# Batch 1's values ahead of w1's second half, another order of the first products, another filler and other places in a kernel of memory attention and a mixture of experts

## The chip, the cores and the metric

The kernel runs on one core of one Trainium2 chip. The time is that of the device in microseconds (us), the median of several runs; smaller is better.

## What is computed

Eight batches of 576 tokens go through an attention over 32 memory slots per head and then through a layer with eight experts, of which each token uses one.

```python
a = exp(phi - max over tokens); a = a / (sum over tokens + 1e-9)
k_m, v_m = einsum('bhsm,bhsd->bhmd', a, k), the same with v
attn = softmax(q @ k_m.T / 8);  x = attn @ v_m          # x: [8, 576, 512]
e(b, s) = argmax(x @ w_gate) if s == 0 or sigmoid(x @ w_local) < 0.5 else e(b, s-1)
out[b, s] = softmax(x @ w_gate)[e] * (relu(x @ w1[e]) @ w2[e])   # w1: 512x1024, w2: 1024x512
```

## The kernel before

For each batch the kernel works with the expert of the batch's first token; which other experts occur is listed along the way, and a loop at the end (`rest`) adds their tokens, if there are any. Since `x` is `attn @ v_m`, the values are multiplied into w1 once per batch: G = v_m @ w1 (`w_pg` makes the product per half of w1, and `w_G` splits it into a high and a low part, `Gh` by ScalarE and `Gl` by VectorE). The first layer (`hidden`) is then attention times G, in three products per head group: `ah`·`Gh`, `ah`·`Gl` and `al`·`Gh`, where `ah` and `al` are the high and low parts of the attention `at`. It first takes 256 tokens in four blocks of 12 products (the first two blocks need the first half of w1, the other two the second half), then 320 tokens in eight blocks of 6. The second layer (`second`, `second_turned`) follows with w2, also in a high and a low part (`w_split`: ScalarE and GpSimd).

Memory and its products. `fetch_phi` and `fetch_kv` load phi, keys and values of a batch; `f_colmax` to `f_exp` make `a`; `f_pkv` ("pkv 0": token groups 0 to 4, "pkv 1": the rest) multiplies it with keys and values; `f_sums` to `f_kvT` normalise and turn the result. All loads are issued by SyncE, in the order of the program.

Order. The kernel is written for a schedule by hand: each engine does its work in the order in which the program names it. `start()` names the work in front of the first block of batch 0: batch 0's memory, its first attention, its expert (`choose`, `expert`), w1 and w2 of that expert (`load1` and `load2`, a half each), batch 1's keys and values, and G of the first half of w1. After that the first and second layer of the batches 0 to 7 follow one another, and all work for the next batches is set between their blocks by the table `PLACES`: for each step and batch a point on a nominal time axis on which each batch has 37.8. The loop at the end runs the blocks, adds each block's nominal length (six products of 256 tokens count 6 x 0.118, of 320 tokens 6 x 0.147, of 512 columns 6 x 0.227) and, after each block, runs all steps whose point has been passed, in the order of their points:

```python
for x in moe(sts[b]):
    now += x
    while places and places[0][0] <= min(now, (b + 1) * END - 0.01):
        _, _, name, n = places.pop(0)
        STEPS[name](sts[n])
```

The four blocks of 256 tokens of batch 0 so end at 1.416, 2.832, 4.248 and 5.664, its first layer at 12.72. Steps that the change touches: "pg 1" and "G 1" (`w_pg` and `w_G` of w1's second half), "pkv 0", "pkv 1", "g pl" and "g lt" (products of the gate and their turning), the softmax of a batch's second half of tokens ("z turn" to "z al", functions `k_turn` to `k_al`), "pl0", "choice" and "expert" (gate of the first token and its expert). "pkv 0" of batch 1 has a filler in front, products of a zero tile into a tile that nobody reads (`warm`).

Of the kernel before, what the change touches and what calls it, by code (L numbers as in the profile page):

```python
# [8 lines left out]
F32 = mybir.dt.float32  # L9
# [17 lines left out]
    "kv": {2: 6.76, 3: 36.1, 4: 68.59, 5: 94.32, 6: 129.4, 7: 168.6},  # L27
    "colmax": {2: 21.1, 3: 55.3, 4: 78.6, 5: 109.2, 6: 147.3, 7: 185.1},
# [8 lines left out]
    "asum": {1: 0.01, 2: 31, 3: 64.8, 4: 92, 5: 127.6, 6: 164.8, 7: 203.2},  # L37
    "pkv 0": {1: 1.34, 2: 30.71, 3: 66.71, 4: 92.5, 5: 127.8, 6: 165.6, 7: 203.7},
    "pkv 1": {1: 4.88, 2: 32.7, 3: 66.71, 4: 94.32, 5: 127.8, 6: 165.6, 7: 203.7},
# [5 lines left out]
    "kv store": {0: 17.59, 1: 15.6, 2: 41.9, 3: 75.4, 4: 98.1, 5: 137.1, 6: 174.4, 7: 212.2},  # L45
    "pgg": {1: 9.9, 2: 44.49, 3: 73.1, 4: 97.61, 5: 135.78, 6: 172.1, 7: 210.8},
    "ggt": {1: 9.9, 2: 44.79, 3: 74.3, 4: 99.7, 5: 135.9, 6: 173.7, 7: 211.5},
# [16 lines left out]
    "choice": {1: 22.9, 2: 54.6, 3: 87.2, 4: 112.5, 5: 149.7, 6: 190.51, 7: 227.3},  # L64
    "expert": {1: 23.1, 2: 54.8, 3: 87.9, 4: 113, 5: 150.2, 6: 190.51, 7: 227.8},
# [38 lines left out]
    "list": {7: 278.9},  # L104
# [8 lines left out]
}  # L113
# [3 lines left out]
def tile_memattn_stickymoe(  # L117
# [12 lines left out]
    nc = tc.nc  # L130
    B, H, S, D = q.shape
    M = phi.shape[3]
    E, DM, F = w1.shape
    P = 128
# [18 lines left out]
    ps_o = ctx.enter_context(tc.tile_pool(name="ps_o", bufs=2, space=PSUM))  # L153
# [153 lines left out]
    def warm(n, cols=512):  # L307

        if not wt or cols < 512:
            wt[0] = ps_o.tile([P, 512], F32, tag="po", name="wp")  # L310
        for _ in range(n):
            if cols > 512:
                nc.tensor.matmul(wt[0], lhsT=zeros, rhs=zeros[:, 0:1].to_broadcast([P, 512]), start=True, stop=True)
                continue
            nc.tensor.matmul(wt[0][:, 0:cols], lhsT=wz[:, 0:P], rhs=wz[:, 0:cols], start=True, stop=True)


# [464 lines left out]
    def w_load1(st, w1e, i, parts=1):  # L782

        w1v = w1e.rearrange("o (h p) f -> p (o h) f", p=P)
        if i == 0:
            st.raw1 = []
        raw = pw.tile([P, HG, F // 2], F32, tag="raw", name="raw1", bufs=3)
        n = F // 2 // parts
        for j in range(parts):
            f0 = F // 2 * i + n * j  # L790
            nc.sync.dma_start(out=raw[:, :, n * j : n * j + n], in_=w1v[:, :, f0 : f0 + n])
        st.raw1.append(raw)

    def w_load2(st, w2e, i):

        w2v = w2e.rearrange("o (c p) d -> p (o c) d", p=P)
        if i == 0:
            st.raw2, st.W2 = [], []
        raw = pw.tile([P, 4, DM], F32, tag="raw", name="raw2", bufs=3)
        for j in (0, 2):  # L800
            nc.sync.dma_start(out=raw[:, j : j + 2], in_=w2v[:, 4 * i + j : 4 * i + j + 2])
        st.raw2.append(raw)
# [258 lines left out]

    def expert(st):

        st.e = nc.values_load(
            st.ei[0:1, 0:1],
            engines=(mybir.EngineType.SP,),
            min_val=0,
            max_val=E - 1,
            skip_runtime_bounds_check_because="an index of the gate's E values",
        )  # L1070

    def load1(st, i, parts=1):
        w_load1(st, w1[bass.ds(st.e, 1)], i, parts)

    def load2(st, i):
        w_load2(st, w2[bass.ds(st.e, 1)], i)

    V = nc.vector
    h, w = pairs
    a, z = PARTS  # L1080
# [25 lines left out]
    def pkv_0(st):  # L1106
        if st.b == 1:
            warm(83, 32)
        f_pkv(st, slice(0, 5))
# [98 lines left out]
    def start():  # L1208
# [50 lines left out]
        expert(s)  # L1259
        load1(s, 0, 2)  # L1260
        load1(s, 1)
        fetch_kv(n, (1,))
        load2(s, 0)
# [75 lines left out]
```

## Time and profile before

| | us |
|---|---|
| runs, median of 3 | 407.85 (407.73 to 408.11) |
| profiled execution, its own time | 406.67 |
| its span, first to last instruction | 404.9 |

The profile shows one execution. Engines: PE is TensorE's matmul, PEld its weight load, DVE VectorE, ACT ScalarE, POOL GpSimd, SP SyncE, which issues the loads. A row of the timeline gives start, duration, engine, line of the kernel, operation, output and inputs by their tile names, shapes and count; in brackets stands the idle time of the engine before it and what ended it. A row of busy windows gives the stretch, its length, the busy time of PE, PEld, DVE, ACT and POOL with the number of instructions, the granted TensorE clock as a share of the full one, the DMA engines' share and GB/s. In the list of waits stand the waiting line, what it waited for, the total, the number and the longest.

In the trace the first block of batch 0 starts at 27.7 us, that of batch 1 at 84.6, that of batch 7 at 359.9, and the last product ends at 398.6.

### The profile page before, as it was taken

What the parts mean: (1) busy time and instruction counts of PE and PEld (TensorE: products, weight loads), DVE (VectorE), ACT (ScalarE), POOL (GpSimd) and SP (SyncE); (2) the same over time, 40 slices, a digit from 0 to 9 for tenths busy, and PEclk for the clock granted to TensorE, in tenths of its full rate; (3) what the DMA queues carried; (4) which work ended last, traced back from release to release, by engine and by line L of the source; (5) the groups of instructions that cost most, each with busy time, mean ns of one, the idle gap of its engine ahead of it and who ended that gap; (6) DMA issues with size and microseconds to landing.
All of it is one profiled execution on the core that took longest, in us unless ns stands there. A gap on an engine that the chain in (4) does not pass through costs nothing.

```text
span 404.9 us, 10638 instructions
## 1 busy us (share of the span) xinstructions
PE 389.3 (96%) x4216; PEld 329.6 (81%) x4216; DVE 286.1 (71%) x718; ACT 177.7 (44%) x436; POOL 151.7 (37%) x164
## 2 busy tenths in 40 slices
PE   7888999999999999999999999999999999999993
PEld 2547878798788877899878997899878996999883
DVE  4588789889977887896877777796867674826300
ACT  2256553446353744337441764245641653255110
POOL 3024442446242851039311771036711741164000
PEclk9999999999999999999999999999999999999998
DMA  7988893989497939899979378944995094302011
GB/s 225 321 296 225 172 378 134 252 197 358 151 305 162 375 107 265 196 389 315 229 198 375 100 202 188 343 189 120 222 223 161 8 307 153 127 0 66 26 54 45
DMA packets 115446, 82.59 MB, mean 204 GB/s; under 512 B 69616, under 2 KB 89088, under 8 KB 115392
## 3 DMA queue, kind: packets, MB, share of 16 engines
q1 hardware_dynamic: 115328, 81.84, 68.3%
q8 instruction: 35, 0.57, 0.6%
q0 software_dynamic: 64, 0.02, 0.2%
q14 instruction: 19, 0.16, 0.1%
HBM read 66.60 MB, written 15.24 MB: 202 GB/s over the span
## 4 chain that ended last, share of the span: by engine, by line
PE 87%; DVE 4%; DMA 4%; SPq 2%; ACT 1%; issue 1%; DVEq 0%; ACTq 0%
PE ph L857 23%; PE po L945 9%; PE po L895 9%; PE po L947 8%; PE po L946 8%; PE po L896 8%; PE po L897 8%; PE pg L824 4%; PE pkv L412 4%; PE psc L533 2%; DMA raw<-in_moe_w_dram 2%; DMA q<-in_q_dram 2%; PE pl L640 1%; DVE h L867 1%; SPq L237 1%; SPq L298 1%
## 5 line engine op out<-in xcount | busy, mean ns | idle before, releaser
L813 POOL TENSOR_TENSOR w2l<-raw,w2h 128x512 fp32r<-128x512 f32 x64 | 82.4, 1307 | 29.1 <-ACT w2h L812 19.3
L857 PE MATMUL ph<-ah,Gh 128*128 128x256 f32 (+1 forms) x256 | 74.2, 305 | 1.2 <-DVE h L867 1.0
L867 DVE SCALAR_TENSOR_TENSOR h<-ph,h 128x320 fp32r<-128x320 f32 (+2 forms) x104 | 52.8, 522 | 31.0 <-ACT h L865 30.3
L857 PE MATMUL ph<-ah,Gl 128*128 128x256 f32 (+1 forms) x256 | 72.1, 296 | 0.1
L945 PE MATMUL po<-h,w2l 128*128 128x320 f32 x224 | 70.8, 316 | 0.0
L946 PE MATMUL po<-h,w2h 128*128 128x320 f32 x224 | 69.2, 309 | 0.0
L947 PE MATMUL po<-h,w2h 128*128 128x320 f32 x224 | 69.2, 309 | 0.0
L865 ACT ACTIVATE h<-ph 128x320 fp32r<-128x320 f32 (+1 forms) x96 | 46.4, 487 | 39.9 <-PE ph L857 39.9
L895 PE MATMUL po<-w2h,h 128*128 128x512 f32 (+1 forms) x152 | 60.0, 394 | 0.0
L896 PE MATMUL po<-w2l,h 128*128 128x512 f32 (+1 forms) x152 | 57.9, 381 | 0.0
L897 PE MATMUL po<-w2h,h 128*128 128x512 f32 (+1 forms) x152 | 57.7, 380 | 0.0
L952 POOL TENSOR_TENSOR oT<-oT,gT 128x320 f32<-128x320 f32 x28 | 20.7, 740 | 95.1 <-DVE oT L951 81.0
L601 POOL TENSOR_TENSOR al<-at,ah 128x576 fp32r<-128x576 f32 (+1 forms) x18 | 23.8, 1327 | 85.9 <-ACT ah L597 75.6
L857 PE MATMUL ph<-al,Gh 128*128 128x256 f32 (+1 forms) x256 | 55.2, 296 | 0.2 <-POOL al L601 0.2
L857 PEld LDWEIGHTS ph<-ah,Gh 128*128 128x128 f32 x256 | 48.4, 189 | 4.9 <-issue 2.1
L857 PEld LDWEIGHTS ph<-ah,Gl 128*128 128x128 f32 x256 | 48.6, 190 | 0.3 <-DVE Gl L839 0.3
L945 PEld LDWEIGHTS po<-h,w2l 128*128 128x128 f32 x224 | 42.1, 188 | 4.4 <-issue 4.0
L812 ACT ACTIVATE w2h<-raw 128x512 fp32r<-128x512 f32 x64 | 38.6, 624 | 9.4 <-PE po L947 8.5
L946 PEld LDWEIGHTS po<-h,w2h 128*128 128x128 f32 x224 | 42.1, 188 | 0.2
L947 PEld LDWEIGHTS po<-h,w2h 128*128 128x128 f32 x224 | 42.1, 188 | 0.0
L857 PEld LDWEIGHTS ph<-al,Gh 128*128 128x128 f32 x256 | 41.4, 190 | 0.4 <-POOL al L601 0.4
L895 PEld LDWEIGHTS po<-w2h,h 128*128 128x128 f32 x152 | 28.6, 188 | 8.2 <-issue 3.0
(163 smaller groups left out, 585.5 us busy)
## 6 DMA issues: line engine op xcount, KB each, us to landing
raw<-in_moe_w_dram SPq DMA_DIRECT2D x34, 512.0 KB, 6.6
raw<-in_moe_w_dram SPq DMA_DIRECT2D x15, 1024.0 KB, 6.2
kv_t<-in_k_dram SPq DMA_DIRECT2D x7, 1152.0 KB, 9.1
kv_t<-in_v_dram SPq DMA_DIRECT2D x7, 1152.0 KB, 11.5
q_t<-in_q_dram SPq DMA_DIRECT2D x112, 72.0 KB, 3.6
att_d<-at SPq DMA_DIRECT2D x8, 576.0 KB, 8.2
out_dram<-oT SPq DMA_DIRECT2D x28, 160.0 KB, 6.4
out_dram<-ot SPq DMA_DIRECT2D x17, 256.0 KB, 4.4
```

The costliest lines, as they stand in the source:

```text
L601: (eng or nc.gpsimd).tensor_tensor(out=st.al[:, gs, ss], in0=st.at[:, gs, ss], in1=st.ah[:, gs, ss], op=ALU.subtract)
L812: nc.scalar.activation(h, src, AF.Copy)
L813: nc.gpsimd.tensor_tensor(out=l, in0=src, in1=h, op=ALU.subtract)
L857: nc.tensor.matmul(pv[:, c - c0], lhsT=lt[:, g, cs], rhs=rt[:, g, s0 : s0 + n], start=(i == 0), stop=(i == 5),)
L865: nc.scalar.activation(hc[:, :, 0:n], pv, AF.Relu)
L867: nc.vector.scalar_tensor_tensor(out=hc[:, :, o : o + z - a], in0=pv[:, :, a:z], scalar=0.0, in1=hc[:, :, a:z], op0=ALU.max, op1=ALU.subtract,
L895: nc.tensor.matmul(po[:, c0:c1], lhsT=h[:, c, th], rhs=hi, start=(c == 0), stop=False)
L896: nc.tensor.matmul(po[:, c0:c1], lhsT=h[:, c, th], rhs=lo, start=False, stop=False)
L897: nc.tensor.matmul(po[:, c0:c1], lhsT=h[:, c, tl], rhs=hi, start=False, stop=(c == FC - 1))
L945: nc.tensor.matmul(po[:, 0:n], lhsT=lo, rhs=h[:, c, 0:n], start=(c == 0), stop=False)
L946: nc.tensor.matmul(po[:, 0:n], lhsT=hi, rhs=h[:, c, 0:n], start=False, stop=False)
L947: nc.tensor.matmul(po[:, 0:n], lhsT=hi, rhs=h[:, c, n : 2 * n], start=False, stop=(c == FC - 1))
```

## The change

In `start()` the load of batch 1's values goes in front of the load of w1's second half. In batch 0, "pg 1", "G 1" and "pkv 0" of batch 1 go from behind the first block to behind the second; the exponential and the sum of the softmax's second half go ahead of "G 1", the steps behind it stay behind; "g pl" goes from behind the fourth block to behind the third, and the first two splits of w2 one block later. The filler of 83 products of 32 columns in bfloat16 becomes one such product and 41 products of 64 rows by 32 columns by one column in FP32 (`burn`). Other points of the table move by little; one definition that stood twice is taken out.

```diff
@@ PLACES
-    "pkv 0": {1: 1.34, 2: 30.71, 3: 66.71, 4: 92.5, 5: 127.8, 6: 165.6, 7: 203.7},
+    "pkv 0": {1: 2.5, 2: 30.71, 3: 66.71, 4: 92.5, 5: 127.8, 6: 165.6, 7: 203.7},
...
-    "pl0": {1: 21.7, 2: 54.5, 3: 86.6, 4: 111.6, 5: 149.4, 6: 190.51, 7: 226.4},
-    "choice": {1: 22.9, 2: 54.6, 3: 87.2, 4: 112.5, 5: 149.7, 6: 190.51, 7: 227.3},
-    "expert": {1: 23.1, 2: 54.8, 3: 87.9, 4: 113, 5: 150.2, 6: 190.51, 7: 227.8},
+    "pl0": {1: 21.7, 2: 54.8, 3: 86.6, 4: 111.6, 5: 149.4, 6: 190.51, 7: 226.4},
+    "choice": {1: 22.9, 2: 54.9, 3: 87.2, 4: 112.5, 5: 149.7, 6: 190.51, 7: 227.3},
+    "expert": {1: 23.1, 2: 55.1, 3: 87.9, 4: 113, 5: 150.2, 6: 190.51, 7: 227.8},
...
-    "z exp": {0: 0.03, 1: 26.8, 2: 54.9, 3: 88.8, 4: 129, 5: 166.2, 6: 203.3, 7: 241.8},
-    "z sum": {0: 0.03, 1: 26.8, 2: 55.4, 3: 88.8, 4: 129.2, 5: 166.6, 6: 203.8, 7: 242.2},
-    "z inv": {0: 0.23, 1: 27.6, 2: 55.4, 3: 88.8, 4: 130.8, 5: 168, 6: 205.6, 7: 244.3},
+    "z exp": {0: 1.5, 1: 26.8, 2: 54.9, 3: 88.8, 4: 129, 5: 166.2, 6: 202.7, 7: 241.8},
+    "z sum": {0: 1.5, 1: 26.8, 2: 55.4, 3: 88.8, 4: 129.2, 5: 166.6, 6: 203.2, 7: 242.2},
+    "z inv": {0: 2.75, 1: 27.6, 2: 55.4, 3: 88.8, 4: 130.8, 5: 168, 6: 205, 7: 244.3},
...
-    "pg 1": {0: 0.13, 1: 32.7, 2: 71.5, 3: 97.6, 4: 139.89, 5: 173, 6: 216.89, 7: 245.61},
-    "G 1": {0: 0.13, 1: 32.8, 2: 71.6, 3: 98.3, 4: 139.89, 5: 175.9, 6: 216.89, 7: 248.3},
-    "g pl": {0: 4.27, 1: 30.72, 2: 61.6, 3: 94.3, 4: 130.8, 5: 168.6, 6: 205.9, 7: 245.6},
+    "pg 1": {0: 2.49, 1: 32.7, 2: 71.5, 3: 97.6, 4: 135.79, 5: 172.11, 6: 210.81, 7: 245.61},
+    "G 1": {0: 2.49, 1: 32.8, 2: 71.6, 3: 98.3, 4: 139.89, 5: 175.9, 6: 216.89, 7: 248.3},
+    "g pl": {0: 3.1, 1: 30.72, 2: 61.6, 3: 94.3, 4: 130.8, 5: 168.6, 6: 205.9, 7: 245.6},
...
@@ tile_memattn_stickymoe
+    def burn(n):
+
+        t = ps_o.tile([P, 512], F32, tag="po", name="wp")
+        for _ in range(n):
+            nc.tensor.matmul(t[0:32, 0:1], lhsT=zeros[0:64, 0:32], rhs=zeros[0:64, 0:1], start=True, stop=True)
...
     def pkv_0(st):
         if st.b == 1:
-            warm(83, 32)
+            warm(1, 32)
+            burn(41)
         f_pkv(st, slice(0, 5))
...
         expert(s)
         load1(s, 0, 2)
+        fetch_kv(n, (1,))
         load1(s, 1)
-        fetch_kv(n, (1,))
         load2(s, 0)
```

The other points that move: "colmax" of batch 4 from 78.6 to 78.9, "pgg" of batch 2 from 44.49 to 44.79, the query loads "q 0" and "q 1" of batches 4 to 7 by 0.4 to 1.3 to earlier, "a inv", "a mul", "a at" and "a ah" of batch 1 to 20.8 (from 18.8, 19.7, 19.7 and 20.5), "z mul" to "z al" of batches 0 and 6 in step with the rows above, "g lt" of batch 0 from 5.1 to 3.1, "split 0" of batch 0 from 2.5 to 3.2 and "split 7" of batch 7 from 270.2 to 274.7.

More of the change, by code (lines that the diff above doesn't have):

```diff
@@ L27 @@
     "kv": {2: 6.76, 3: 36.1, 4: 68.59, 5: 94.32, 6: 129.4, 7: 168.6},
-    "colmax": {2: 21.1, 3: 55.3, 4: 78.6, 5: 109.2, 6: 147.3, 7: 185.1},
+    "colmax": {2: 21.1, 3: 55.3, 4: 78.9, 5: 109.2, 6: 147.3, 7: 185.1},
     "pm": {2: 24.1, 3: 59.1, 4: 84, 5: 113.7, 6: 151.8, 7: 189.6},
@@ L45 @@
     "kv store": {0: 17.59, 1: 15.6, 2: 41.9, 3: 75.4, 4: 98.1, 5: 137.1, 6: 174.4, 7: 212.2},
-    "pgg": {1: 9.9, 2: 44.49, 3: 73.1, 4: 97.61, 5: 135.78, 6: 172.1, 7: 210.8},
+    "pgg": {1: 9.9, 2: 44.79, 3: 73.1, 4: 97.61, 5: 135.78, 6: 172.1, 7: 210.8},
     "ggt": {1: 9.9, 2: 44.79, 3: 74.3, 4: 99.7, 5: 135.9, 6: 173.7, 7: 211.5},
[2 rows of a table removed]
[2 rows of a table added]
     "a qT 0": {1: 6.2, 2: 39, 3: 73.1, 4: 98.4, 5: 135.1, 6: 173.01, 7: 213.2},
@@ L1060, in rest @@
             nc.sync.dma_start(out=rows, in_=ot[0:n])
[L1062 to L1076, printed above, removed]
     V = nc.vector
```

26 rows, old and new, of the table PLACES are left out of this document.

## The prediction

> **What bounds the kernel now.** I read the page's head first, then the busy time of one long window, then the list of waits.
>
> ```profile
> span 404.9 us, 10638 instructions
> ...
> PE 389.3 (96%) x4216; PEld 329.6 (81%) x4216; DVE 286.1 (71%) x718; ACT 177.7 (44%) x436; POOL 151.7 (37%) x164
> ...
> 84.60:398.70 314.10, 312.19 (x3096) 272.24 (x3094) 221.06 (x553) 140.54 (x345) 122.01 (x103) 1.00 0.66 197
> ...
> PE ph L857 <- DVE h L867: 1.0, 1, 1.0
> PE pkv L412 <- issue: 0.9, 1, 0.9
> ...
> PE pl L616 <- DVE at L593: 0.6, 1, 0.6
> ```
>
> From 84.6 us (first first-layer product of batch 1) to 398.7 us (last product) TensorE is busy for 312.19 of 314.10 us; of the missing 1.91 us, the two waits of 1.0 and 0.6 us are nearly all. So TensorE sets the time: what delays its stream in batch 0 arrives at the end undiminished, and a step moved inside that window gains only if it removes one of these two waits. The ends inside batch 0 are read from TensorE's own timeline (start, duration, line, tiles, count, idle time before).
>
> ```profile
> 29.90 0.40 PE L857 MATMUL ph<-al,Gh 128*128 128x256 f32 x2
> 30.48 1.09 PE L824 MATMUL pg<-raw,kvT 64*32 64x512 f32 x16 [0.18 <-DMA raw<-in_moe_w_dram]
> 31.51 2.24 PE L315 MATMUL wp<-wz 128*128 128x32 bf16 x83
> 34.66 1.36 PE L412 MATMUL pkv<-kv_t,phi_t 64*32 64x128 f32 x80 [0.91 <-issue]
> 35.95 0.39 PE L857 MATMUL ph<-ah,Gh 128*128 128x256 f32 x1
> ...
> 40.46 0.74 PE L640 MATMUL pl<-at,ggt 128*32 128x160 f32 x16
> 41.13 1.16 PE L412 MATMUL pkv<-kv_t,phi_t 64*32 64x128 f32 x64
> 42.02 0.29 PE L427 MATMUL pkv<-ones,asum 64*32 64x1 f32 x16
> 42.25 0.41 PE L857 MATMUL ph<-ah,Gh 128*128 128x320 f32 x1
> ```
>
> The order is block 1 of the first layer (to 30.3), pg 1, 83 filler products, pkv 0, blocks 2 to 4 (35.95 to 40.46), g pl, pkv 1 with its sums, and from 42.25 the 320-token half. Between filler and pkv 0 stands an idle 0.91 us that the view calls "issue". What ends it is a transfer: SyncE's queue and the landings of its loads show it (the first row is the chain's wait for w1's second half; then the issues of batch 1's values and of w2's two pieces, and from issue to landing of the one and of the two).
>
> ```profile
> 22.60 7.75 DMA raw<-in_moe_w_dram
> ...
> 23.03 0.50 SPq L237 DMA_DIRECT2D kv_t<-in_v_dram  x1
> 23.72 1.11 SPq L801 DMA_DIRECT2D raw<-in_moe_w_dram  x2
> ...
> DMA to landing us min/median/max: 11.5/11.5/11.5
> ...
> DMA to landing us min/median/max: 12.8/13.7/14.6
> ...
> 29.00:30.50 1.50, 1.11 (x11) 0.93 (x11) 1.50 (x3) 0.16 (x1) 1.12 (x2) 1.00 1.02 384
> 30.50:32.00 1.50, 1.50 (x36) 0.66 (x36) 1.47 (x4) 1.47 (x3) 0.00 (x0) 1.00 1.04 396
> 32.00:33.50 1.50, 1.50 (x67) 1.50 (x63) 1.43 (x4) 0.23 (x1) 1.19 (x1) 1.00 1.05 399
> ```
>
> w1's second half, issued at 22.60, lands at 30.35; the values, issued at 23.03, land 11.5 us later, at 34.53, and pkv 0 starts at 34.66. The last two numbers of a window are the DMA engines' busy share and GB/s: the share is 1.02 to 1.05 all this time, so the loads stand in line and land in the order of issue.
>
> **The change, part by part.** (1) *The loads.* The values go in front of w1's second half. In a full queue that exchanges two landings, not the end of the pair: the values (8 x 576 x 64 floats, 1.18 MB, against 1.05 MB of w1) take the place of 30.35 and are there near 31, and w1's second half takes that of 34.53. From both sides: what was moved after 30.35, 1.18 MB at 399 GB/s, needs 3.0 us, so 33.4 at the earliest; at the latest it comes with the next piece, w2's first, at 23.72 + 12.8 = 36.5. I take 34.53, the measured end of the same bytes.
>
> (2) *The order on TensorE.* A step placed at x runs after the block whose end passes x; blocks 1 to 4 end at 1.416, 2.832, 4.248 and 5.664. pg 1, filler and pkv 0 (2.49, 2.5) therefore come behind block 2, g pl (3.1) behind block 3, pkv 1 (4.88) stays behind block 4. So TensorE does blocks 1 and 2 up to about 31.8 and then stands before pg 1, which needs w1's second half: idle from 31.8 to 34.65. It is in order; pkv 0, whose values have long landed, is queued behind the waiting pg 1, and so are blocks 3 and 4, both value products and the whole rest. The first wait has not gone, it stands before another step at the same time of day.
>
> From 34.66 to 42.25 the kernel before did pkv 0, three blocks, g pl, pkv 1, sums: 7.59 us. The changed one has from the same moment:
> - pg 1 in addition: 31.51 - 30.48 = 1.03 us;
> - the filler in addition, which stood ahead of the wait and now stands behind it: see (3);
> - two blocks instead of three. Twelve products take 1.44 (36 took 35.95 to 40.46 = 4.51, of which 36 x 0.12 = 4.32 by their spacing and 0.19 is the entry after small tiles). With g pl between blocks 3 and 4 the entry is paid twice: 2 x 1.44 + 2 x 0.19 = 3.26 instead of 4.51, that is -1.25 us.
>
> (3) *The filler.* It was 83 products of 32 columns; it is one of these and 41 FP32 products of 64 rows by 32 columns by one column, all on the same part of the array and into one tile. An FP32 product shows as two records (line 427 issues 8 products and shows x16), so 82 records. The trace has none such in one place; the nearest rows are the old filler, (2.24 - 0.18) / 82 = 25 ns apart, the four records of line 616 and line 517's, and line 427's, of the same shape but spread over eight places of the array:
>
> ```profile
> 24.58 0.43 PE L517 MATMUL pq<-ident,q0e 32*128 32x32 f32 x4
> ...
> L517 PE MATMUL pq<-ident,q0e 32*128 32x32 f32 x4 | 0.4, 227 | 0.0
> ...
> 104.67 0.25 PE L616 MATMUL pl<-ggt,at 128*1 128x8 f32 x4 [0.64 <-DVE at L593]
> ...
> L616 PE MATMUL pl<-ggt,at x4: 169/169/171, 104.7 to 104.7; 128*1 128x8 f32 x4
> ...
> L427 PE MATMUL pkv<-ones,asum x16: 163/166/167, 42.0 to 42.2; 64*32 64x1 f32 x16
> ```
>
> Line 616: (0.25 - 0.17) / 3 = 27 ns. Line 427: (0.29 - 0.165) / 15 = 8 ns. Line 517, with 128 columns of weights: (0.43 - 0.227) / 3 = 68 ns. I take 25 ns, since line 616 and the old filler stay in one place as this does: 83 x 25 = 2.08 us, between 0.7 (8 ns) and 5.6 us (68 ns). [...]
>
> Could the filler be hidden? Block 3 needs G 1, which ScalarE and VectorE make of pg 1.
>
> ```profile
> 33.24 0.97 DVE L568 TENSOR_TENSOR sc<-sc,mx 128x576 f32<-128x576 f32 x1
> ...
> 34.83 1.06 ACT L837 ACTIVATE Gh<-pg 128x512 fp32r<-128x512 f32 x2
> ...
> 35.63 1.28 DVE L839 TENSOR_TENSOR Gl<-pg,Gh 128x512 fp32r<-128x512 f32 x2
> ...
> 38.12 0.78 DVE L593 STREAM_TRANSPOSE at<-sc 128x576 f32<-128x576 f32 x1
> ```
>
> Exponential and sum of the softmax are now placed ahead of G 1; in the kernel before, too, they stood ahead of line 837's and line 839's rows, which began at 34.83 and 35.63, and what they wait for, the subtraction, ends at 34.2. So both engines are free when pg 1 ends at 35.7. One eviction (0.53 plus some 0.15 to start) and two subtractions (1.28) end 2.0 us after pg 1, near 37.7. pkv 0's 1.30 us covers most of that; of the filler only 0.7 us is cover, the other 1.4 us is on the path. Before, `at` was whole (38.12 + 0.78) 2.0 us after the subtractions' end (35.63 + 1.28); so it is now at 39.7, and g pl, which reads it, comes at 40.6: no wait.
>
> Sum for batch 0: 1.03 + 2.08 - 1.25 = **+1.86 us**; the 320-token half would start at 44.1.
>
> (4) *pl0 of batch 2* goes from 54.5 to 54.8. Its ticks are 54.61 and 55.97 (37.8 + 12.72 + multiples of 1.362), so it runs six products of 0.23 us later. VectorE's transpose, for which it waits, ends at 104.6:
>
> ```profile
> 103.84 0.78 DVE L593 STREAM_TRANSPOSE at<-sc 128x576 f32<-128x576 f32 x1
> 106.08 0.75 DVE L563 TENSOR_REDUCE mx<-sc 128x18 f32<-128x576 f32 x1
> 106.75 0.15 DVE L629 MAX8 m<-pl 1x8 f32<-1x8 f32 x1
> ```
>
> Without the wait pl0 would now come at 104.0 + 1.4 = 105.4: **-0.64 us**. The choice behind it already stands behind the maximum that ends at 106.8 on VectorE, so SyncE's wait for the expert, and w1's load behind that, come no later.
>
> (5) *The other places.* colmax of batch 4 (78.6 to 78.9) stays on the tick 79.85 and in the same place on VectorE; the 1.0 us wait at line 857 that its long reduction causes stays. The earlier pg 1 of batches 4 and 6 leaves a neighbour and gains one: pg beside psc takes 215.63 - 214.75 = 0.88, alone 1.03, so 0.15 either way.
>
> ```profile
> 214.75 1.09 PE L824 MATMUL pg<-raw,kvT 64*32 64x512 f32 x16
> 215.63 0.69 PE L533 MATMUL psc<-qT,kvT 64*32 64x288 f32 x16
> ```
>
> The earlier query loads stand ahead of weights on SyncE by one tick at most, z exp and split 7 move on engines that are 44% and 37% busy: nothing, hidden by the gapless TensorE; if that cover were gone, one such step late costs at most its own 0.6 to 1.3 us. The duplicate definitions are dead text.
>
> Sum: +1.86 - 0.64 = +1.2 us. The profiled execution took 406.67 us itself (span 404.9), so 407.9 for one like it; the runs' median of 407.85 lies 1.2 above that one, which I leave as it is: **409.0 us**.
>
> **The rivals.** *A cheap filler* (0.18): if equal tiles also start 8 ns apart, the filler is 0.7 us; block 3 then starts at 37.7, with G 1, and not at 39.0: batch 0 loses 1.86 - 1.3 = 0.5, which line 616's 0.64 outweighs: 407.7, not slower. It decides at 20 ns a record, below which the sum stays under what can be measured; at 10 ns it is nought. For it speaks line 427's identical shape, against it line 616. *The second half lands early* (0.15): if its last packets do not lag as the values' did, pg 1 starts at 33.5 and 1.1 us comes back: 407.9; for it speaks the 399 GB/s, against it that the same bytes ended at 34.53. Both together give 406.6. *The clock falls* (0.07): the filler no longer stands in the idle time, so TensorE has nothing for 2.7 us.
>
> ```profile
> 395.00:398.70 3.70, 3.60 (x31) 3.40 (x29) 0.00 (x0) 0.53 (x2) 0.00 (x0) 1.00 0.14 49
> 398.70:402.70 4.00, 0.00 (x0) 0.00 (x0) 0.00 (x0) 0.41 (x1) 0.00 (x0) 1.00 0.12 37
> 402.80:404.90 2.10, 0.00 (x0) 0.00 (x0) 0.00 (x0) 0.00 (x0) 0.00 (x0) 0.50 0.05 16
> ```
>
> At the end the granted clock stayed 1.00 for 4 us without a product and then fell to 0.50. 2.7 us is less, so I expect no fall; if it fell, the next 3 us of products at half speed would cost 3 more: 412. [...] *The later waits go* (0.08): if the shift also removes the 1.0 us before line 857 and the waits of batch 0's second layer, the sum is -0.3 or lower: 406.7.
>
> **How the numbers follow.** Forecast as summed: 0.52. A measurement of this kernel tells 0.2%, that is 0.8 us, from no change: faster is below 407.0, slower above 408.7. Slower: the forecast but for a tail of its low side (0.43) and the clock (0.07), 0.50. Faster: the later waits and the two cheap cases together, 0.14. Within: 0.36. The range takes the cheap filler and the early landing at its lower end, 407.3, and at its upper a filler of 45 ns a record or a landing with w2's piece, 1.7 to 1.9 more: 410.8.
>
> **What would show it.** Right: values landing near 31, pg 1 starting at 34.6 behind some 2.7 us of idle time, the new filler 2 us long between pg 1 and pkv 0, the 320-token half starting near 44.1 instead of 42.25, no wait before line 616 near 106, and from there the same stream shifted by 1.2 us. Wrong: a filler of 0.7 us, pg 1 before 34, a wait before block 3, a granted clock under 1.00 near 35 us, or new waits behind 85 us.

## The result and the profile after

| | before | after |
|---|---|---|
| runs, median | 407.98 us (6) | 413.68 us (6, 410.48 to 414.32) |
| ratio, 95% interval | | 1.0128 [1.0098, 1.0158] |
| profiled execution, its own time | 406.67 | 413.57 |
| its span | 404.9 | 411.8 |

The changed kernel is slower by 1.3%. The ratio leaves out two of the six runs before, at 413.71 and 414.57, which fell into a slower state. In what follows the changed kernel's line numbers are higher by 6 than in the kernel before (857 is 863, 824 is 830, 412 is 418). From the head of its page, the busy time, and the clock that TensorE was granted in 40 slices, in tenths:

```profile
span 411.8 us, 10638 instructions
...
PE 394.1 (96%) x4214; PEld 333.1 (81%) x4216; DVE 286.8 (70%) x718; ACT 177.7 (43%) x436; POOL 151.8 (37%) x164
...
PEclk9996899999999999999999999999999999999999
```

The work is the same and TensorE is busy for 394.1 us instead of 389.3: its products themselves took longer, and the one slice with a 6 says where. TensorE's timeline of batch 0, to be set beside the rows that the prediction shows of before:

```profile
28.25 0.39 PE L863 MATMUL ph<-ah,Gh 128*128 128x256 f32 x1
...
31.70 0.40 PE L863 MATMUL ph<-al,Gh 128*128 128x256 f32 x2
34.10 1.40 PE L830 MATMUL pg<-raw,kvT 64*32 64x512 f32 x16 [2.01 <-DMA raw<-in_moe_w_dram]
35.44 0.21 PE L315 MATMUL wp<-wz 128*128 128x32 bf16 x1
35.58 4.48 PE L321 MATMUL wp<-zeros 64*32 64x1 f32 x81
...
39.97 2.32 PE L418 MATMUL pkv<-kv_t,phi_t 64*32 64x128 f32 x73
42.22 0.58 PE L863 MATMUL ph<-ah,Gh 128*128 128x256 f32 x1
...
45.07 0.74 PE L646 MATMUL pl<-at,ggt 128*32 128x160 f32 x16
45.74 0.39 PE L863 MATMUL ph<-ah,Gh 128*128 128x256 f32 x1
...
47.37 1.16 PE L418 MATMUL pkv<-kv_t,phi_t 64*32 64x128 f32 x64
...
48.49 0.41 PE L863 MATMUL ph<-ah,Gh 128*128 128x320 f32 x1
```

The order is the forecast one, and there is an idle time before pg 1, of 2.01 us where some 2.7 had been forecast. But the filler, line 321, takes 4.48 us (35.44 to its last record at 39.92) where 2.08 had been summed, pkv 0 behind it 2.30 (to 42.22) instead of 1.30, and block 3 (42.22 to 45.07) 2.85 while block 4 behind it (45.74 to 47.37) takes 1.63. The busy windows, cut where the granted clock changes (the third number from the end is the clock, the first one after the length the busy time of PE); first two rows of the kernel before in the same stretches, then those of the changed kernel:

```profile
31.39:34.77 3.38, 2.47 (x100) 2.28 (x100) 2.75 (x5) 1.37 (x3) 2.38 (x2) 1.00 1.06 381
34.77:38.18 3.41, 3.41 (x98) 3.21 (x96) 3.12 (x7) 1.61 (x4) 0.93 (x3) 1.00 0.84 107
```

```profile
31.39:34.77 3.38, 1.37 (x22) 0.72 (x21) 3.31 (x6) 1.87 (x4) 2.02 (x2) 1.00 1.04 389
34.77:38.18 3.41, 3.41 (x58) 2.71 (x51) 3.09 (x7) 1.59 (x3) 1.29 (x3) 0.50 1.06 132
38.18:41.59 3.41, 3.41 (x103) 3.29 (x109) 1.23 (x2) 0.68 (x1) 1.35 (x2) 0.50 0.85 138
41.59:45.01 3.42, 3.42 (x40) 2.88 (x28) 0.00 (x0) 0.00 (x0) 0.20 (x1) 0.50 0.59 93
45.01:48.50 3.49, 3.49 (x110) 3.03 (x109) 1.40 (x4) 2.66 (x6) 2.13 (x2) 1.00 0.92 227
```

Behind a window in which TensorE had work for 1.37 of 3.38 us the clock is at half for three windows of 3.41 us, 34.77 to 45.01, and exactly there lie the long products. The rest of the way, in stretches of TensorE's stream in the two profiled executions:

| stretch | before | after | change |
|---|---|---|---|
| to the first block of batch 0 | 27.67 | 28.25 | +0.58 |
| from there to the 320-token half | 14.58 | 20.24 | +5.66 |
| to batch 1 | 42.36 | 43.14 | +0.78 |
| batch 1 | 47.82 | 47.83 | +0.01 |
| batch 2 | 49.06 | 49.44 | +0.38 |
| batches 3 to 7, to the last product | 217.11 | 217.18 | +0.07 |

Together 7.48 us; behind the last product 0.58 come back, which gives the 6.90 between the two profiled executions. The one of before lay 1.3 us below its median, so the medians differ by 5.7. The first of these rows is not the change's: in the fourteen profiles of these experiments the first block starts anywhere from 27.67 to 30.57, and at 29.62 in the kernel before with only pl0's place moved, whose program is the same up to there. From batch 1 on TensorE is as dense as before:

```profile
91.60:406.10 314.50, 312.79 (x3096) 271.69 (x3094) 221.04 (x554) 140.38 (x344) 122.16 (x103) 1.00 0.65 197
```

So two things were to be settled: what brings the clock down near 35 us, and what the +0.78 of batch 0's later part is. In the list of waits there is one that the kernel before had only at 0.3 us, and for another reason:

```profile
PE psc L539 <- DVE qT L508: 1.1, 1, 1.1
```

### The profile page after: what moved, and what is told of

It reads as the page before. It is cut to its first block, busy times and chain, and to the rows that moved or that the text cites. A ratio compares the mean times of both kernels' runs of the same rounds, so it can differ in the third digit from the quotient of the medians.

```text
span 411.8 us, 10638 instructions
## 1 busy us (share of the span) xinstructions
PE 394.1 (96%) x4214; PEld 333.1 (81%) x4216; DVE 286.8 (70%) x718; ACT 177.7 (43%) x436; POOL 151.8 (37%) x164
## 4 chain that ended last, share of the span: by engine, by line
PE 83%; DVE 6%; DMA 5%; SPq 3%; ACT 1%; issue 1%; DVEq 0%; ACTq 0%
PE ph L863 22%; PE po L951 9%; PE po L953 8%; PE po L952 8%; PE po L901 8%; PE po L903 7%; PE po L902 7%; PE pkv L418 4%; PE pg L830 4%; DMA raw<-in_moe_w_dram 2%; PE psc L539 2%; DMA q<-in_q_dram 2%; DVE h L873 2%; SPq L237 1%; PE pl L646 1%; DMA kv_d<-kvT 1%
## 5 line engine op out<-in xcount | busy, mean ns | idle before, releaser
L958 POOL TENSOR_TENSOR oT<-oT,gT 128x320 f32<-128x320 f32 x28 | 20.8, 742 | 95.5 <-DVE oT L957 95.5
L863 PEld LDWEIGHTS ph<-al,Gh 128*128 128x128 f32 x256 | 41.9, 192 | 0.4 <-POOL al L607 0.4
```

The source lines that it names most:

```text
L863: nc.tensor.matmul(pv[:, c - c0], lhsT=lt[:, g, cs], rhs=rt[:, g, s0 : s0 + n], start=(i == 0), stop=(i == 5),)
```

## The experiments

"Ratio" is always to the kernel before, in the same set of runs; the clock named beside it is the median over the runs of the mean granted clock of one run (the changed kernel: 0.9845, each run between 0.983 and 0.986; the kernel before 0.994 to 0.995).

### The filler put into the idle time

The 83 old products ahead of batch 0's pg 1, none behind it:

```diff
 def pkv_0(st):
-    if st.b == 1:
-        warm(1, 32)
-        burn(41)
...
+def pg_1(st):
+    warm(83, 32)
+    w_pg(st, 1)
```

> The changed kernel with 83 bfloat16 products of 32 columns ahead of pg 1, in TensorE's idle time, and no filler ahead of pkv 0. Theory A (an idle time of 2 us ahead of pg 1 lowers the granted clock for 10 us, and that makes most of the loss; the filler behind the wait makes the rest): granted clock 0.996 or more, no half clock near 35 us, the 320-token half starts near 41.5 us instead of 48.5, time near 406.5. Theory B (the clock falls whatever stands in the gap; only the filler's length on the path counts): clock 0.99 or less, time as without any filler, near 410.

Measured: 409.46 us, ratio 1.0046 [1.002, 1.0072], clock 0.993. Its timeline:

```profile
31.81 2.24 PE L315 MATMUL wp<-wz 128*128 128x32 bf16 x83
34.11 1.09 PE L830 MATMUL pg<-raw,kvT 64*32 64x512 f32 x16
...
39.25 0.73 PE L646 MATMUL pl<-at,ggt 128*32 128x160 f32 x14 [0.28 <-DVE at L599]
...
42.66 0.41 PE L863 MATMUL ph<-ah,Gh 128*128 128x320 f32 x1
```

pg 1 starts when it did, at 34.11, but the 320-token half comes at 42.66 instead of 48.49, and no half clock is granted until the kernel's end: 4.2 us of the median come back (3.3 by the two ratios). The 406.5 us that were expected did not come. The same with the new filler (one product and `burn(41)` ahead of pg 1):

> The same, but the filler in the gap is the changed kernel's: one product of 32 columns and 41 FP32 products of 64 rows, 32 columns and one column. If any product keeps the clock: 406.5 and a clock of 0.996 or more, as with the whole-array filler. If products that use an eighth of the array hardly count as activity: the half clock near 35 us stays, and the time is that without any filler, 409 to 410.5.

409.29 us, ratio 1.0047 [1.0024, 1.007], clock 0.994: the same. Its profiled execution still lost one window, and its busy windows show something that the medians don't:

```profile
31.36:34.77 3.41, 3.41 (x87) 3.34 (x86) 3.30 (x7) 1.96 (x4) 1.75 (x2) 1.00 1.05 387
34.78:38.20 3.42, 3.42 (x87) 2.10 (x87) 1.88 (x4) 1.77 (x3) 1.55 (x3) 0.50 0.92 151
```

In the first window PE is busy throughout, 0.85 us with the first layer and 2.4 us with the one-place products (from 32.33 on; "one-place" since all of them use the same 64 by 32 places of the array), and the next one is at half clock all the same.

### Old filler behind the idle time, and no filler

```diff
-            warm(1, 32)
-            burn(41)
+            warm(83, 32)
```

> The changed kernel with the former filler of 83 bfloat16 products of 32 columns in the new filler's place, ahead of pkv 0 and behind pg 1. If the kind of filler counts as activity: the clock falls near 34.8 but is back one window of 3.4 us later, near 38.2, so some 3 us are saved: near 410.5, mean clock 0.994. If the kind is all the same: 413.7 and a clock of 0.985 as in the changed kernel.

410.28 us, ratio 1.006 [1.0031, 1.0089], clock 0.9925. The place is that of the changed kernel, 83 records as well, 2.17 us long in the profile, and the idle time is left open; only the products are wide ones (128 by 128 places). The loss is less than half that of the changed kernel, whose six runs are all at 0.983 to 0.986. The clock of these ten lies between 0.982 and 0.999; runs of the kernel before spread as widely (0.983 to 0.999), so it is not known in how many of the ten this idle time cost a window. The profiled one lost none, with more work left in the window of the idle time:

```profile
30.37:33.78 3.41, 2.03 (x22) 1.62 (x28) 3.31 (x6) 2.34 (x4) 1.23 (x1) 1.00 1.05 396
33.78:37.20 3.42, 3.42 (x145) 2.79 (x132) 3.27 (x6) 1.66 (x3) 2.10 (x4) 1.00 1.11 189
```

(The idle time in this profile was 1.38 us, in the changed kernel's 2.01; the transfer differs from run to run, so that one pair of profiles does not separate its length from the kind of filler.) Without any filler:

> The changed kernel without any filler. Theory A: the gap ahead of pg 1 stays, so the clock falls as before near 34.8 us; the 4.4 us of filler go, block 3 waits for G 1 and runs at half clock; 409 to 410.5, mean clock 0.985 to 0.993. Theory C (the filler of small products itself lowers the clock): clock 0.996 or more and time near 406.5.

413.19 us, ratio 1.0141 [1.0092, 1.019], above both times that were expected; but the clock is 0.993, and the 320-token half starts already at 42.24. This kernel loses its time elsewhere. Its waits of TensorE from 88 to 300 us:

```profile
PE pkv L433 <- issue: 1.7, 1, 1.7
PE pkv L418 <- issue: 1.5, 1, 1.5
...
PE po L901 <- issue: 0.5, 1, 0.5
```

Of this kind the changed kernel has one there, of 0.3 us. Batches 2 to 5 take 50.79, 47.72, 45.91 and 46.31 us instead of the 49.06, 45.8, 45.14 and 46.0 of the kernel before: 4.7 us more. So the filler did a second thing that its name hides; the last part of the experiments follows this up.

### The loads

The changed kernel with the loads in their old order, and the kernel before with nothing but the new order of the loads:

```diff
-        fetch_kv(n, (1,))
         load1(s, 1)
+        fetch_kv(n, (1,))
```

> The changed kernel with w1's second half loaded ahead of batch 1's values again; order on TensorE and filler as changed. Theory A (the loss comes from the idle time ahead of pg 1, which the exchange of the loads makes): w1's half lands near 30.4 us, pg 1 follows block 2 without an idle time, granted clock 0.996 or more, the 320-token half starts near 41.5 us, and with the later wait of 1 us at psc the time is near 408. If the filler of small products lowers the clock by itself: clock 0.99 or less and 411 or more.

> The kernel before with only the two loads exchanged. Theory A: TensorE stands idle behind block 1 for 3.5 us, longer than in the changed kernel; the clock falls in nearly every run (mean 0.985 to 0.994), and three blocks, pg 1, filler and pkv 0 all stand behind the wait: 412 to 416. If the exchange costs only what stands behind the wait and no clock: 410 and a clock of 0.996.

The first: 408.21 us, ratio 1.0036 [1.0004, 1.0067], clock 0.994; no half clock, though the same new filler stands behind the same pg 1:

```profile
31.91 1.13 PE L830 MATMUL pg<-raw,kvT 64*32 64x512 f32 x16
...
33.09 2.72 PE L321 MATMUL wp<-zeros 64*32 64x1 f32 x81
...
42.59 0.41 PE L863 MATMUL ph<-ah,Gh 128*128 128x320 f32 x1
```

The second: 412.69 us, ratio 1.0132 [1.0088, 1.0176], clock 0.9835. Here pg 1 stands behind the first block, the idle time is 2.6 us, and the old filler does not help:

```profile
29.54:32.96 3.42, 3.42 (x27) 2.61 (x28) 2.44 (x5) 1.33 (x5) 2.51 (x3) 0.50 1.02 382
32.96:36.37 3.41, 0.80 (x12) 0.36 (x18) 2.39 (x6) 1.74 (x3) 1.21 (x1) 1.00 1.07 372
36.37:39.78 3.41, 3.41 (x99) 2.29 (x83) 2.66 (x5) 1.66 (x3) 2.11 (x4) 0.50 0.76 94
39.78:43.20 3.42, 3.42 (x100) 3.22 (x98) 1.86 (x4) 0.37 (x1) 0.00 (x0) 1.00 0.57 93
```

Behind the window with 0.80 us of work stands one at half; behind that one, which held pg 1 and the wide filler, the clock is back, where the changed kernel needed three. The 0.9835 is not the work of this idle time alone: the profile has two more windows at half clock ahead of it, from 12.48 us and, the first row, from 29.54 us, the latter behind a window with 1.62 us of work in which pg 0 waits 1.56 us for w1's first half; why these waits are longer here was not followed up. One window at half is 0.004 of a run's mean clock (half of 3.41 in 411.8 us), so the changed kernel's 0.986 stands for its three and the kernel's end. With the kernels above this is the answer on the clock: the idle time before pg 1 with one-place products behind it costs one per cent of the clock in each of six runs; without the idle time, or with wide products or none behind it, the median clock is 0.9925 to 0.994, about that of the kernel before. Whether the clock then stays up or falls for one window in some of the runs, these medians cannot tell.

### The place of pl0

The kernel before with only the places of "pl0", "choice" and "expert" of batch 2:

```diff
-    "pl0": {1: 21.7, 2: 54.5, 3: 86.6, 4: 111.6, 5: 149.4, 6: 190.51, 7: 226.4},
+    "pl0": {1: 21.7, 2: 54.8, 3: 86.6, 4: 111.6, 5: 149.4, 6: 190.51, 7: 226.4},
```

> The kernel before with only the places of pl0, choice and expert of batch 2 moved as in the change. The prediction's term: the wait of 0.64 us goes and nothing comes for it, 0.6 us faster, ratio 0.9985. What the changed kernel's trace suggests: VectorE's column maximum, behind the transposes, is late next, so pm waits 0.2 us, and pl0 apart from psc costs another entry of small tiles: ratio 1.000.

408.02 us, ratio 1.001 [0.9985, 1.0034]: no gain. In its profile from line 533's psc (105.36) to the products of line 640 (115.11) it takes 9.75 us, as in the kernel before (103.32 to 113.07), and 9.76 in the changed one, though the wait of 0.64 is gone. The rows of the changed kernel show what took its place:

```profile
110.34 0.72 PE L539 MATMUL psc<-qT,kvT 64*32 64x288 f32 x16
...
112.24 0.40 PE L903 MATMUL po<-w2h,h 128*128 128x512 f32 x1
112.57 0.25 PE L622 MATMUL pl<-ggt,at 128*1 128x8 f32 x4
112.74 0.50 PE L901 MATMUL po<-w2h,h 128*128 128x512 f32 x1
113.08 0.39 PE L902 MATMUL po<-w2l,h 128*128 128x512 f32 x1
...
117.30 0.33 PE L362 MATMUL pm<-ident,cm 128*128 128x128 f32 x1 [0.18 <-DVE cm L326]
```

psc and pl had shared one change from wide products to small ones and back. Now each has its own: 0.33 from the product ahead of pl to pl and 0.34 from the first product behind it to the second, instead of the 0.23 of the stream, 0.2 together. Then pm comes early and waits 0.18 for VectorE's maxima, and the rest goes around the two pm products in the same way (0.65, with that wait in it, and 0.42 from the product ahead of each to the one behind, instead of 0.26 and 0.29).

### Batch 0's second half: VectorE behind GpSimd

The 1.1 us before line 539 begins with one small operation of VectorE, `pr<-pe,es` (line 746, before: 740). First the row of the kernel before and its neighbour on GpSimd, then those of the changed kernel, from the timelines of all engines:

```profile
52.29 0.17 DVE L740 TENSOR_TENSOR pr<-pe,es 32x18 f32<-32x18 f32 x1
...
52.46 1.29 POOL L813 TENSOR_TENSOR w2l<-raw,w2h 128x512 fp32r<-128x512 f32 x1 [7.00 <-ACT w2h L812]
```

```profile
58.50 1.30 POOL L819 TENSOR_TENSOR w2l<-raw,w2h 128x512 fp32r<-128x512 f32 x1 [7.09 <-ACT w2h L818]
58.55 1.29 DVE L746 TENSOR_TENSOR pr<-pe,es 32x18 f32<-32x18 f32 x1
```

The same 32x18 operation takes 0.17 us when it starts 0.17 ahead of GpSimd's product and 1.29 when it starts 0.05 behind it; it ends 0.04 behind it. Over the fourteen profiles it is 1.29 or 1.30 us in the eleven in which it starts 0.03 to 0.05 behind GpSimd's product, and 0.17 in the three in which it starts 0.17 to 0.28 ahead of it; what holds it up no run shows. But the collision is not the change's: the kernel before with only pl0's place of batch 2 moved, whose batch 0 is that of the kernel before, has it in its profile:

```profile
53.52 1.30 POOL L813 TENSOR_TENSOR w2l<-raw,w2h 128x512 fp32r<-128x512 f32 x1 [6.42 <-ACT w2h L812]
53.56 1.30 DVE L740 TENSOR_TENSOR pr<-pe,es 32x18 f32<-32x18 f32 x1
```

There, too, line 533 then waits 1.1 us, and the stretch from the 320-token half to batch 1 takes 43.12 us (43.53 to 86.65), near the changed kernel's 43.14. The profiled execution of the kernel before was one that escaped it. Two edits of the kernel with the filler in the idle time were tried, each one point of the table:

```diff
-    "split 0": {0: 3.2, 1: 37.9, 2: 72.4, 3: 111.9, 4: 147.6, 5: 184.3, 6: 222, 7: 258.6},
+    "split 0": {0: 2.5, 1: 37.9, 2: 72.4, 3: 111.9, 4: 147.6, 5: 184.3, 6: 222, 7: 258.6},
```

> The kernel with the filler in the gap, and the first split of w2 of batch 0 back at its old place (2.5). Theory D: VectorE's small operation at line 746 took 1.29 us because it began 0.04 us behind a split on GpSimd and had to let that finish; it came late since splits on GpSimd ran 1 us longer beside it. With the split back, that chain is 0.2 us earlier, line 746 takes 0.2 us, psc waits 0.5 us instead of 1.5: 1 us below the kernel with the filler in the gap, near 408.4. If the late transposes have another cause: the same 409.5.

409.55 us, ratio 1.0039 [1.0013, 1.0064], line 746 still at 1.29 us: the new place of the first split is not the cause.

```diff
-    "split 4": {0: 11.6, 1: 45.8, 2: 77.5, 3: 116.6, 4: 152.2, 5: 195.7, 6: 228.6, 7: 264.9},
+    "split 4": {0: 12.5, 1: 45.8, 2: 77.5, 3: 116.6, 4: 152.2, 5: 195.7, 6: 228.6, 7: 264.9},
```

> The kernel with its whole filler of 83 bf16 products ahead of pg 1, with GpSimd's split 4 of batch 0 a tick later (12.5 instead of 11.6). Theory A (VectorE's small multiplication of line 746 in batch 0 takes 1.29 us instead of 0.17 because a GpSimd product of the split starts just ahead of it, and both cannot run at once): with GpSimd's start off that point it takes 0.2 us, the wait of line 539 for the transposed queries falls from 1.1 to under 0.3 us, and the median falls by 0.8 to 1.0, to 408.5. Theory B (the long duration belongs to VectorE's own operation or its other neighbours): still 1.29 us and the wait still 1.1. Theory C: the short duration comes, but the wait moves to the second layer, whose weights are then split 0.5 to 1.3 us later, and the median stays at 409.5.

407.75 us, ratio 1.0002 [0.9972, 1.0031]. The operation is short again:

```profile
52.61 0.17 DVE L746 TENSOR_TENSOR pr<-pe,es 32x18 f32<-32x18 f32 x1
...
52.89 1.29 POOL L819 TENSOR_TENSOR w2l<-raw,w2h 128x512 fp32r<-128x512 f32 x1 [6.63 <-ACT w2h L818]
```

The wait of line 539 falls to 0.2 us, as expected; half a microsecond of it comes back in the second layer (its first 30 products take 7.54 instead of 7.03), and batch 0 as a whole gets 0.6 shorter in the profile. The median fell by 1.7. That this is more than the edit explains is shown by the same edit on the kernel with the old loads:

> The changed kernel with the loads in their old order (no idle time before pg 1) and GpSimd's split 4 of batch 0 a tick later: the two repairs together. Theory A (the two losses are separate, and the collision of VectorE's line 746 with GpSimd's split is worth what the same edit was worth behind the filled gap): line 746 at 0.17 us, the wait of line 539 near 56 us under 0.4 instead of 1.3, the span 0.6 to 1.1 below the 406.4 of the kernel with the old loads alone, and a median of 406.7 to 407.6, ratio 0.997 to 1.000: level with or a little below the kernel before. Theory B (the 1.7 us between those two medians was mostly the disturbance of single runs): line 746 short, but the median stays at 408.0 to 408.4. Theory C (the start of the split follows the batch, and falls on line 746 again): 1.29 us still.

408.41 us, ratio 1.0029 [1.0003, 1.0056]: the operation short, the wait at 0.2, batch 0 shorter by 0.96 in the profile, and the median where it was (408.21). So the collision and its 1.1 us are shown; what it is worth in the median lies somewhere between 0 and 1.7 us and is not settled, nor how many runs of the kernel before have it. This kernel, both repairs together, was the one meant to beat the kernel before; it does not.

### How many products, and the value products in the idle time

The filler in the idle time with 42 instead of 83 products:

> The kernel with its whole filler of 83 bf16 products ahead of pg 1, but 42 of them instead of 83: 41 instructions fewer on TensorE's queue, and half the idle time open. [...] If half the idle time is enough to bring the clock down, half clock is seen from 34.8 on and pg 1 to the 320-token half takes over 9.5 us.

413.8 us, ratio 1.0145 [1.0092, 1.0199], clock 0.995. The idle time is half open and the 320-token half earlier (42.22), yet the waits are back, two of the three at other places; from its list for the whole span:

```profile
PE pkv L418 <- issue: 3.4, 3, 1.4
```

Batches 2 to 5 take 49.97, 45.82, 46.36 and 47.41 us. A wait of this kind behind 88 us thus comes and goes with the number of products that do nothing at 32 us: 1.7, 1.5 and 0.5 us without filler, two of together 2.0 with half of it, one of 0.3 in the changed kernel; the edit of the change keeps that number (83 records for 83). What TensorE waits for there no run shows.

Last, pkv 0 ahead of pg 1, with 35 filler products, and pkv 1 with the other 48 behind pg 1:

```diff
-    "pkv 0": {1: 2.5, 2: 30.71, 3: 66.71, 4: 92.5, 5: 127.8, 6: 165.6, 7: 203.7},
-    "pkv 1": {1: 4.88, 2: 32.7, 3: 66.71, 4: 94.32, 5: 127.8, 6: 165.6, 7: 203.7},
-    "g pl": {0: 3.1, 1: 30.72, 2: 61.6, 3: 94.3, 4: 130.8, 5: 168.6, 6: 205.9, 7: 245.6},
-    "g lt": {0: 3.1, 1: 30.9, 2: 62.2, 3: 94.3, 4: 132.9, 5: 170.1, 6: 208.5, 7: 247.7},
+    "pkv 0": {1: 2.48, 2: 30.71, 3: 66.71, 4: 92.5, 5: 127.8, 6: 165.6, 7: 203.7},
+    "pkv 1": {1: 2.495, 2: 32.7, 3: 66.71, 4: 94.32, 5: 127.8, 6: 165.6, 7: 203.7},
+    "g pl": {0: 4.87, 1: 30.72, 2: 61.6, 3: 94.3, 4: 130.8, 5: 168.6, 6: 205.9, 7: 245.6},
+    "g lt": {0: 5.1, 1: 30.9, 2: 62.2, 3: 94.3, 4: 132.9, 5: 170.1, 6: 208.5, 7: 247.7},
```

> The changed kernel with the loads in its new order, but batch 1's first value products ahead of pg 1 instead of behind it (their values land near 31.3, w1's second half near 34), so that they and 35 of the bf16 filler products stand in TensorE's idle time; the other 48 come behind batch 0's g pl, whose products and remaining value products keep their old order behind block 4. Theory A (the idle time and what stands behind it are the loss, and the 80 value products and half the filler are the right thing to put in the idle time): no record of half clock between 30 and 45 us, pg 1 at 34.1 as in the kernel with all 83 products ahead of it, behind it only pg 1 and blocks 3 and 4, so the 320-token half starts near 41.2 to 41.9 instead of 42.66, and the median is near 408.2 (ratio 0.999 to 1.003), which with clean clock is 0.7 to 1.4 below the kernel with the filler ahead. Theory B (batch 0 is not what sets the rest, waits further on give it back): the 320-token half earlier as said, but the median stays at 409.3. Theory C (the second layer's products or the eviction of G 1 become late): block 3 waits for G 1 by 0.5 to 1.5 us, and nothing is won in batch 0.

410.49 us, ratio 1.007 [1.0039, 1.0101], clock 0.991. The 320-token half starts at 43.0, not at 41.2 to 41.9: of that 0.6 is the first block's later start, and from there it takes 14.19 us, hardly less than the 14.42 with all filler ahead, since the 48 products behind pkv 1 (37.37 to 39.10) stand on the path. Behind it the wait for the turned memory has grown from 0.8 to 1.7 us, with a window at half clock behind that:

```profile
46.97:50.38 3.41, 1.75 (x27) 1.49 (x27) 3.26 (x11) 1.57 (x6) 0.89 (x1) 1.00 1.02 332
50.38:53.79 3.41, 3.41 (x15) 3.41 (x14) 3.02 (x16) 1.06 (x4) 0.00 (x0) 0.50 1.05 406
```

None of the three theories foresaw this wait and its window.

## Why the prediction was wrong, point by point

**The step that failed** is the dismissal of the third rival: "2.7 us is less, so I expect no fall". It was read from the end of the trace, where the clock stayed for 4 us without a product. That row was read as a length of idle time that the clock tolerates. The windows show another thing: in the changed kernel's profile the clock changes at 34.77, 45.01 and 410.24 us, 10.24 and 365.23 us apart, that is 3 and 107 times 3.413, and it falls behind a window with 1.37 us of work. The last product of before ended at 398.7, and the clock fell at 402.75; counted back by the same 3.41 us the window from 399.34 was empty, and the one ahead of it held 2.67 us of work. Read so, the 4 us were 0.7 us of a busy window and one empty window; they show no idle time that the clock tolerates. In the changed kernel the idle time of 2.01 us lay wholly in one window, left 1.37 us of work in it, and the clock fell at its end; with the idle time filled by wide products, or taken away, no window is lost there. A window without any work was not needed: 1.37 of 3.38 us of work were not enough here.

**Its size** was too small as well. The forecast priced a fall at 3 us; no run shows that term, which was the author's estimate (the trace of before ends 2.1 us behind its fall). Here the fall lasted three windows, 10.24 us, and the loss is that of the rows: pg 1 1.34 - 1.03 = 0.31, the filler 4.48 - 2.71 = 1.77 (2.71 is what it takes at full clock, see below), pkv 0 2.30 - 1.30 = 1.00, block 3 2.85 - 1.63 = 1.22, in sum 4.30 us. That it lasted three is put down to the filler, which is argued and not shown by itself: with wide products behind it the fall of the kernel before with the new loads (36.37) lasted one window; a window with 2.4 us of one-place products was followed by half clock in the kernel with the same filler in the idle time; and at half clock the filler is longer, so that it and the small pkv products fill the second window too.

**The order was right, the filler's term too small.** In the kernel with the old loads the filler stands at full clock and without a wait: from line 315's product at 32.97 to pkv 0's main part at 35.68 it takes 2.71 us, 32 ns from record to record, instead of 2.08 by 25 ns; at half clock 4.48 us, 54 ns. The value lies near the old filler and line 616, as taken, and the cheap filler (8 ns) is ruled out, but the step lost 0.63. From pg 1's start to the 320-token half the forecast had 44.1 - 34.66 = 9.44 us. It took 48.49 - 34.10 = 14.39; less 4.30 for the clock and 0.63 for the filler that makes 9.46: what is left of the order's sum holds to 0.02.

**The landings** were right in kind. From the chain of work that ended last (start, duration):

```profile
22.61 1.31 SPq L237
...
24.12 9.85 DMA raw<-in_moe_w_dram
```

w1's second half landed at 33.97, not at 34.53; the values, 8.7 us after their issue, near 31.3. pg 1 so starts 0.56 earlier than forecast (34.10), between the forecast and its rival of an early landing. With this the start of the 320-token half is accounted for: the forecast 1.86, 0.63 more for the filler, 4.30 for the clock, 0.56 less for the landing make 6.23, and it starts 48.49 - 42.25 = 6.24 us later. That 5.7 of it arrive in the medians agrees with "what delays its stream in batch 0 arrives at the end". That without the fall the forecast of +1.2 would have been near is partly luck: 1.86 + 0.63 - 0.56 makes 1.9, and the 0.64 of pl0, below, did not come off it.

**The filler's cover** was named rightly (0.7 us). With the filler ahead of pg 1, block 3 takes 2.22 us and g pl, which waits for `at`, 1.40, instead of 1.62 and 0.67 behind the wide filler: of what is won by taking the filler off the path, 1.3 us are given back to steps that it had covered.

**pl0** was wrong: -0.64 forecast, nothing measured, alone (1.001) and in the change. The wait went as forecast; "TensorE sets the time" was taken to mean that a wait removed is a gain, without the price of the second change between wide and small products and without VectorE's maxima, which were late next.

**The other places** had been summed as "nothing, hidden by the gapless TensorE". No run shows that they cost anything: the +0.78 of batch 0 is what VectorE's line 746 behind GpSimd leaves of its 1.1 us of wait, and the kernel before with only pl0's place moved has that too. What the step overlooked is that the stream is not gapless in the second half of batch 0, where a shift of some tenths between VectorE and GpSimd decides on this wait.

## What to carry to other kernels

Price a transfer wait on TensorE by the clock as well: ask how much wide work is left in each 3.41 us around it, the step in which the clock changed in these profiles; a gap of 2 us with one-place products behind it cost 4.3 more here. A filler belongs into the gap, ahead of the waiting instruction; the two kinds made the same median there (409.46 and 409.29), but behind the gap the wide one cost less (410.28 against 413.68). Before a wait is counted as a gain, look for the small products that had stood in it together. And set a second profile of the unchanged program beside the first before a difference between two profiles is put down to an edit.

## What had not been expected of the hardware

- The granted clock changes on a grid of 3.41 us (10.24 and 365.23 us between its changes in the changed kernel's profile). It fell to half behind windows with 0.80, 1.37, 1.62, 1.75 and 2.11 us of work, and behind one busy for all its 3.41 us, of which 2.4 were one-place products. Busy time alone does not order the windows: the clock stayed full behind 2.03 us of work (the kernel with the old filler behind the idle time, 30.37 to 33.78) and fell behind 2.11 us (the kernel with pkv 0 ahead of pg 1, 19.66 to 23.08). That it goes by how much of the array works is the author's estimate from the one window of one-place products; where the bound lies was not measured.
- TensorE's waits called "issue" in batches 2 to 5 (1.7, 1.5 and 0.5 us, 4.7 us in all with what follows) come and go with the number of do-nothing products far ahead of them: none of over 0.4 us there with 83, two of together 2.0 us behind 88 us with 42, the three named with 0.
- A VectorE operation of 0.17 us took 1.29 us when it started 0.05 us behind a GpSimd product, and 1.29 or 1.30 in ten more profiles where it started 0.03 to 0.04 behind.
- The kernel before, too, loses windows in some executions: one with only pl0's place moved (mean clock 0.989, against 0.997 in the profiled execution of the kernel before) was at half clock from 12.5 to 15.9 and from 22.8 to 26.2 us, ahead of everything that the change touches.
